# K on ScalarE's DMA queue, V and the queries on SyncE's: an attention kernel with one load queue or two

## The chip, the cores and the metric

The kernel runs on one core of one Trainium2 chip. A core has five engines with an instruction stream each: TensorE (PE, matrix products), VectorE (DVE), ScalarE (ACT), GpSimd (POOL) and SyncE (SP). They wait for each other on semaphores. Data comes from the chip's memory (HBM) into the on-chip buffer (SBUF) by 16 DMA engines; an instruction stream issues a transfer into its queue, the transfer is then spread over the 16 engines, and a semaphore tells when it has landed. The metric is the device time of one execution in microseconds (us); the number given is the median of the runs.

## The reference

```python
B, H, Sq, Skv, Dh = 8, 16, 16, 2048, 256        # q: B,H,Sq,Dh   k, v: B,H,Skv,Dh   all bf16

def reference(q, k, v):
    scale = q.shape[-1] ** -0.5
    scores = jnp.einsum('bhqd,bhkd->bhqk', q, k) * scale
    attn = _softmax(scores, axis=-1)
    return jnp.einsum('bhqk,bhkd->bhqd', attn, v)
```

There are 128 heads. Each has only 16 queries, but 2048 keys and values of 256 numbers. K and V are 134 MB each and are read once; queries and results are 1 MB each.

## The kernel before

**Tiles.** Eight heads make a group; there are G = 16 groups. The K of a group is loaded as four tiles of 2 MB, `K(4g)` to `K(4g+3)`, each 128 partitions by 32 tokens by 256 numbers, so that a partition reads 16 KB in one row. V is loaded in the same way as `V(4g)` to `V(4g+3)`. That gives NP = 64 loads of K and 64 of V. The last V is cut into four pieces of 16, 8, 4 and 4 tokens.

**Buffers.** `KN` holds raw K in R_KN = 3 slots, `KB` transposed K in R_KB = 3 slots, `VB` holds V in R_V = 5 slots. A load of K(i) waits until the second half of the transpose of K(i-3) is done; a load of V(j) waits until the product that uses V(j-5) is done.

**What happens to a group.** VectorE transposes a K tile in 32x32 blocks, in two halves (`kt`, L128). TensorE multiplies it with the prepared queries into the scores in PSUM (`qk`, L136, 8 products for each half). When all four tiles are in, VectorE takes the maximum (`max`, L142), ScalarE the exponentials in two halves (`exp`, L146), and VectorE transposes them (`pt`, L151) and forms the reciprocal of the sum (L348 to L351). TensorE multiplies with V (`pv`, L161): `pv(g,0)` uses V(4g) and V(4g+1), `pv(g,1)` the other two. ScalarE and VectorE scale and add the result (`evac_a`, L287, and `evac_b`, L295), and ScalarE issues the store of 64 KB (L176). The queries are loaded once (L228), and brought into the form that `qk` needs by TensorE (`qprep`, L113) and ScalarE (`qwb`, L121), two groups ahead.

**Order.** Each engine's stream is written out by hand as a list of jobs, and an engine does its jobs strictly in that order; `emit_stream` puts the waits in front of each. TensorE does, for group g: qk(4g), qk(4g+1), pv(g-1,0), qk(4g+2), qk(4g+3), pv(g-1,1), qprep(g+2). In the last group it does three qk ahead of pv(14,0), then qk(63) and pv(14,1), and then the last group's value products one tile at a time (`pv_last`, L170). ScalarE does, for group g: exp, qwb(g+2), evac_a(g-1), store(g-1). VectorE does kt(4g+1) to kt(4g+3), max(g), the first half of kt(4g+4), pt(g), the sums, the second half of kt(4g+4), and evac_b(g-1).

**Loads.** SyncE issues all loads, in the order of the list `seq`: K0, the queries, K1, K2, K3, and from then on K(i) followed by V(i-4). At the end the list runs K60, V56, K61, K62, V57, K63, V58 to V63. Since SyncE works in order, a K load that waits for its slot also holds up the V loads behind it.

Of the kernel before, what the change touches and what calls it, by code (L numbers as in the profile page):

```python
# [12 lines left out]
R_KN = 3  # L13
# [12 lines left out]
def bass_standalone__softmax_full_bidir__sampling_kernel(  # L26
# [11 lines left out]
    NP = 4 * G  # L38
# [7 lines left out]
    with ExitStack() as es:  # L46
# [30 lines left out]
        def J(eng, cls, emit, deps=(), dma=None):  # L77
            deps = [d for d in deps if d is not None]
            if dma is not None:
                jb = _Job(eng, cls, emit, deps, dma[0], dma[1], 16)  # L80
            else:
                if (eng, cls) not in counters:
                    counters[(eng, cls)] = [ec(nc.semaphore("c_%s_%s" % (eng, cls))), 0]
                c = counters[(eng, cls)]
                c[1] += 1
                jb = _Job(eng, cls, emit, deps, c[0], c[1])
            order[eng].append(jb)
            return jb
# [28 lines left out]
        def emit_qwb(eng, g):  # L117
            for a in range(4):
                dv = QW[32 * a:32 * a + 32, g % 2, 0, 0, :]
                sv = XP_ps[32 * a:32 * a + 32, 0, :]  # L120
                ins = eng.activation(ap_of(dv, dv.offset + 32 * a, [[8 * 128 + 1, 2], [128, 8], [2, 16]]),  # L121
                                     ap_of(sv, sv.offset + 16 * a, [[64, 2], [128, 8], [1, 16]]),
                                     ACTF.Copy, scale=scale)
            return ins
# [20 lines left out]
        def emit_exp(eng, g, h):  # L145
            return eng.activation(P_sb[:, 1024 * h:1024 * h + 1024],  # L146
                                  S_ps[:, 2 * h:2 * h + 2, :].rearrange("p c n -> p (c n)"), ACTF.Exp,
                                  bias=negm[:, g:g + 1], scale=1.0, accum_out=lsum[:, g, h:h + 1])
# [43 lines left out]
        for j in range(NP):  # L192
            g, r = j // 4, j % 4
            v_of.append((2 * g + r % 2, r // 2) if g < last else (2 * g + r // 2, r % 2))
        seq = []
        for i in range(NP):
            seq.append(("k", i))
            if i == 0:
                seq.append(("q", 0))
            if 4 <= i < NP - 3:  # L200
                seq.append(("v", i - 4))
            elif i == NP - 2:
                seq.append(("v", i - 5))
        seq += [("v", j) for j in range(NP - 6, NP)]

        j_k, j_v, j_kt, j_qk, j_pv = {}, {}, {}, {}, {}
        j_qwb, j_qprep, j_exp, j_pt, j_max, j_rab = {}, {}, {}, {}, {}, {}
# [2 lines left out]

        def k_load(i):
            s = i % R_KN
            return J("sp", "ld", lambda eng: eng.dma_start(
                KN[:, s], ku[i // 2, :, PT_TOK * (i % 2):PT_TOK * (i % 2) + PT_TOK, :]),
                [("kt", i - R_KN, 1) if i >= R_KN else None], dma=(sem_kn[s], 16 * (i // R_KN + 1)))

        def v_load(j, a, n, sem):
            s = j % R_V
            u, h = v_of[j]
            return J("sp", "ld", lambda eng: eng.dma_start(  # L220
                VB[:, s, a:a + n, :], vu[u, :, PT_TOK * h + a:PT_TOK * h + a + n, :]),
                [("pvuse", j - R_V) if j >= R_V else None], dma=sem)

        for what, i in seq:
            if what == "k":
                j_k[i] = k_load(i)
            elif what == "q":
                j_q = J("sp", "ld", lambda eng: eng.dma_start(QR[:], qg), dma=(sem_q, 16))  # L228
            elif i < NP - 1:
                j_v[i] = [v_load(i, 0, PT_TOK, (sem_v[i % R_V], 16 * (i // R_V + 1)))]  # L230
            else:
                parts, a = [], 0
                for x, n in enumerate(tail):
                    sem = ec(nc.semaphore("s_vt%d" % x))
                    parts.append(v_load(i, a, n, (sem, 16)))
                    a += n
                j_v[i] = parts
# [5 lines left out]
        def qwb(g):  # L243
            if g < G:
                j_qwb[g] = J("act", "qwb", lambda eng: emit_qwb(eng, g),
                             [("qprep", g), j_qwz, ("qk", 4 * g - 5, 1) if g >= 2 else None])
# [20 lines left out]
        def pv_last(r):  # L267
            g = last
            j = 4 * g + r
            u, h = v_of[j]  # L270
            a = 0
            for x, jv in enumerate(j_v[j]):
                n = PT_TOK if r < 3 else tail[x]
                j_pv["l", r] = J("pe", "pv", lambda eng, a=a, n=n: emit_pv1(
                    eng, g, u % 2, PT_TOK * h + a, PT_TOK * h + a + n, j % R_V, PT_TOK * h, g % 2 if u % 2 == 0 else 2),
                    [("pt", g, 0), ("pt", g, 1), ("eb", g - 2) if g >= 2 else None, jv])
                a += n

        def softmax_act(g):
            for h in range(2):  # L280
                j_exp[g, h] = J("act", "exp", lambda eng, h=h: emit_exp(eng, g, h),
                                [("max", g), ("pt", g - 1, h) if g else None])

        def evac_a(g):
            if g >= 0:
                dep = ("pvl", 1) if g == last else ("pv", g, 1)
                j_ea[g] = J("act", "ea", lambda eng: eng.activation(  # L287
                    O_tmp[:], O_ps[:, g % 2, 0:D], ACTF.Copy, scale=rab[:, g, 0:1]),
                    [dep, ("rab", g), ("eb", g - 1) if g else None])
# [9 lines left out]
        def store(g):  # L299
            if g >= 0:  # L300
                j_st[g] = J("act", "st", lambda eng: emit_store(eng, g), [("eb", g)],
                            dma=(sem_st[g % 2], 16 * (g // 2 + 1)))
# [19 lines left out]
        for r in range(4):  # L322
            if r == 3:
                J("pe", "warm", lambda eng: emit_warm(eng, 6), [("qwb", last)])
            pv_last(r)

        qwb(0)
        qwb(1)
        for g in range(G):
            softmax_act(g)  # L330
            qwb(g + 2)
            evac_a(g - 1)
            store(g - 1)
# [101 lines left out]
```

## Time and profile before

| | |
|---|---|
| runs | 656.22, 656.55, 656.96 us; median 656.55 |
| span of the profiled execution | 655.0 us |
| moved by the DMA | 271.34 MB, 414 GB/s over the span |
| SyncE's queue (q1) | 269.49 MB, 97.1% of 16 engines |
| ScalarE's queue (q10, the stores) | 1.05 MB, 0.6% |
| busy: TensorE, VectorE, ScalarE | 511.1, 376.3, 74.3 us |

The profiled execution has a span of 655.0 us from its first to its last instruction, 1.55 us less than the median of the runs. In the rows of groups, a row gives line, engine, operation, tiles and count, then the busy time and the mean time of one in ns, then the idle time of the engine just ahead of these instructions and what ended it. In rows of the timeline the first number is the start in us from the beginning of the span, the second the duration of the merged instructions, and brackets give the idle time ahead and what ended it. "SPq" and "ACTq" are instructions that issue a transfer on SyncE's or ScalarE's queue.

### The profile page before, as it was taken

The page shows a single profiled execution, that of the slowest core. Times are in us where ns is not written, and L with a number is a line of the kernel's source. Part 1 is how long each engine was busy: PE and PEld are TensorE (multiplying, and loading weights), DVE is VectorE, ACT ScalarE, POOL GpSimd, SP SyncE. Part 2 cuts the span into 40 slices and gives each one's busy share as a digit, 9 for nine tenths or more (in the row PEclk, how much of TensorE's full clock was granted, in tenths as well). Part 3 has the DMA queues.
Part 4 walks back from the last instruction along what each step waited for, and adds up shares of the span by engine and source line. Part 5 has one row for each costly group of instructions (what it writes and reads, how often), then busy time and mean ns, then how long its engine had stood idle before and what let it go on. Part 6 is the DMA issues. An engine that isn't in the chain of part 4 may idle for free.

```text
span 655.0 us, 12512 instructions
## 1 busy us (share of the span) xinstructions
PE 511.1 (78%) x5894; PEld 215.9 (33%) x5894; DVE 376.3 (57%) x242; ACT 74.3 (11%) x145; POOL 0.7 (0%) x6
## 2 busy tenths in 40 slices
PE   1868987867978777887878868689776878877886
PEld 1323332323333333332333323233322333322355
DVE  3884656557475573754746546574754837548520
ACT  2020201102011020200202002020200202001010
POOL 0000000000000000000000000000000000000000
PEclk9969988989988999888899979998998998879989
DMA  9999999999999999999999999999999999999982
GB/s 341 427 429 428 425 426 429 425 428 426 426 428 424 429 427 428 426 427 428 426 425 429 425 430 425 427 427 425 427 428 427 426 428 425 429 426 427 428 352 75
DMA packets 21747, 271.34 MB, mean 414 GB/s; under 512 B 2368, under 2 KB 4416, under 8 KB 5312
## 3 DMA queue, kind: packets, MB, share of 16 engines
q1 hardware_dynamic: 19392, 269.49, 97.1%
q10 hardware_dynamic: 2304, 1.05, 0.6%
q8 instruction: 46, 0.75, 0.5%
q14 instruction: 5, 0.04, 0.0%
HBM read 269.48 MB, written 1.05 MB: 413 GB/s over the span
## 4 chain that ended last, share of the span: by engine, by line
DMA 55%; PE 28%; DVE 12%; ACT 3%; issue 2%; SPq 0%; DVEq 0%
DMA KN<-in_k_dram 51%; PE O_ps L161 14%; PE S_ps L136 10%; DVE KB L128 10%; DMA VB<-in_v_dram 4%; ACT QW L121 2%; PE O_ps L170 2%; DVE negm L142 1%; DVE PT L151 1%; PE XP_ps L113 1%; ACT O_tmp L287 0%; PE XP_ps L180 0%; DVE rab L351 0%; DVE rinv L350 0%; DVE O_fin L295 0%
## 5 line engine op out<-in xcount | busy, mean ns | idle before, releaser
L128 DVE STREAM_TRANSPOSE KB<-KN 128x2048 f32<-128x2048 f32 x128 | 289.8, 2293 | 194.5 <-DMA KN<-in_k_dram 194.5
L136 PE MATMUL S_ps<-KB,QW 128*128 128x512 bf16 x1024 | 275.2, 422 | 120.4 <-DVE KB L128 119.2
L161 PE MATMUL O_ps<-VB,PT 32*32 32x512 bf16 x3840 | 214.0, 376 | 3.9 <-DMA VB<-in_v_dram 3.9
L136 PEld LDWEIGHTS S_ps<-KB,QW 128*128 128x128 bf16 x1024 | 99.3, 104 | 289.6 <-DVE KB L128 153.3
L161 PEld LDWEIGHTS O_ps<-VB,PT 32*32 32x32 bf16 x3840 | 94.9, 92 | 120.9 <-issue 18.4
L146 ACT ACTIVATE P_sb<-S_ps,negm 128x1024 bf16<-128x1024 f32 x32 | 35.4, 1110 | 497.4 <-DVE negm L142 497.4
L142 DVE TENSOR_REDUCE negm<-S_ps 128x1 f32<-128x2048 f32 x16 | 36.7, 2292 | 48.5 <-PE S_ps L136 48.5
L151 DVE STREAM_TRANSPOSE PT<-P_sb 128x1024 bf16<-128x1024 bf16 x32 | 37.3, 1204 | 1.3 <-ACT P_sb L146 1.3
L121 ACT ACTIVATE QW<-XP_ps 32x256 bf16<-32x256 bf16 x64 | 28.7, 448 | 48.8 <-PE XP_ps L113 48.2
L295 DVE SCALAR_TENSOR_TENSOR O_fin<-O_ps,rab,O_tmp 128x256 bf16<-128x256 f32 x16 | 7.5, 471 | 29.7 <-PE O_ps L170 18.0
L113 PE MATMUL XP_ps<-ident,QR 128*32 128x128 bf16 x512 | 10.9, 232 | 13.7 <-DMA QR<-in_q_dram 11.8
L170 PE MATMUL O_ps<-VB,PT 32*32 32x256 bf16 x512 | 14.8, 268 | 3.1 <-issue 3.1
L170 PEld LDWEIGHTS O_ps<-VB,PT 32*32 32x32 bf16 x512 | 13.2, 92 | 4.8 <-issue 4.1
L113 PEld LDWEIGHTS XP_ps<-ident,QR 128*32 128x32 bf16 x512 | 8.0, 102 | 19.9 <-DMA QR<-in_q_dram 11.8
L287 ACT ACTIVATE O_tmp<-O_ps,rab 128x256 f32<-128x256 f32 x16 | 7.6, 474 | 18.4 <-PE O_ps L161 10.2
L146 ACT ACTIVATION_READ_ACCUMULATOR P_sb<-S_ps,negm 128x1 f32 x32 | 6.3, 196 | 0.0
L351 DVE TENSOR_SCALAR rab<-mask,rinv 128x2 f32<-128x2 f32 x16 | 3.7, 229 | 0.6
L350 DVE RECIPROCAL rinv<-ltot 128x1 f32<-128x1 f32 x16 | 2.6, 164 | 0.5
L186 DVE MEMSET QW<- 128x2048 f32 x1 | 1.8, 1765 | 1.2 <-PEq L420 1.2
L348 DVE TENSOR_REDUCE ltot<-lsum 128x1 f32<-128x2 f32 x16 | 1.8, 113 | 0.0
L121 ACT ACT_TABLE_LOAD x1 | 1.3, 1283 | 3.1 <-DVE QW L186 3.1
L180 PE MATMUL XP_ps<-QR,ident 128*128 128x512 bf16 x6 | 1.5, 381 | 0.0
(8 smaller groups left out, 1.6 us busy)
## 6 DMA issues: line engine op xcount, KB each, us to landing
KN<-in_k_dram SPq DMA_DIRECT2D x64, 2048.0 KB, 24.9
VB<-in_v_dram SPq DMA_DIRECT2D x63, 2048.0 KB, 29.5
out_dram<-O_fin ACTq DMA_DIRECT2D x16, 64.0 KB, 9.5
VB<-in_v_dram SPq DMA_DIRECT2D x1, 1024.0 KB, 8.7
VB<-in_v_dram SPq DMA_DIRECT2D x1, 512.0 KB, 9.6
VB<-in_v_dram SPq DMA_DIRECT2D x2, 256.0 KB, 9.9
QR<-in_q_dram SPq DMA_DIRECT2D x1, 0.5 KB, 10.4
```

The source lines that it names most:

```text
L113: ins = eng.transpose(XP_ps[32 * a:32 * a + 32, bp, :], ap_of(qv, qv.offset + 64 * b + par, [[2, 32]]), ident[:], tile_position=(0, 32 * a))
L121: ins = eng.activation(ap_of(dv, dv.offset + 32 * a, [[8 * 128 + 1, 2], [128, 8], [2, 16]]), ap_of(sv, sv.offset + 16 * a, [[64, 2], [128, ...
L128: return eng.transpose(KBf[:, i % R_KB].rearrange("p t i -> p (t i)")[:, n * h:n * h + n], KNf[:, i % R_KN].rearrange("p t i -> p (t i)")[ ...
L136: ins = eng.matmul(S_ps[:, 2 * half + c, :], QW[:, g % 2, Gh, bp, :], ap_of(kb0, kb0.offset + 64 * b + par, [[D, 16], [2, 32]]), start=(Gh ...
L142: return eng.tensor_reduce(out=negm[:, g:g + 1], in_=S_ps[:].rearrange("p c n -> p (c n)"), axis=AX.X, op=ALU.max, negate=True)
L146: return eng.activation(P_sb[:, 1024 * h:1024 * h + 1024], S_ps[:, 2 * h:2 * h + 2, :].rearrange("p c n -> p (c n)"), ACTF.Exp, bias=negm[ ...
L151: return eng.transpose(PT[:, g % 2].rearrange("p t x -> p (t x)")[:, 1024 * h:1024 * h + 1024], P_sb[:, 1024 * h:1024 * h + 1024])
L161: ins = eng.matmul(O_ps[pr, g % 2, :], PT[pr, g % 2, t, :], rhs, start=(t == 0), stop=(t == NT - 1), tile_position=(32 * a, 32 * a))
L170: ins = eng.matmul(O_ps[pr, bank, D * Gh:D * Gh + D], PT[pr, g % 2, t, :], VB[pr, s, t - base, :], start=(t == 0), stop=(t == NT - 1), til ...
L287: j_ea[g] = J("act", "ea", lambda eng: eng.activation(O_tmp[:], O_ps[:, g % 2, 0:D], ACTF.Copy, scale=rab[:, g, 0:1]), [dep, ("rab", g), ( ...
L295: j_eb[g] = J("dve", "eb", lambda eng: eng.scalar_tensor_tensor(out=O_fin[:, g % 2, :], in0=O_ps[:, bank, D:2 * D], scalar=rab[:, g, 1:2], ...
L351: j_rab[g] = J("dve", "sm", lambda eng, g=g: eng.tensor_scalar(out=rab[:, g, :], in0=mask[:], scalar1=rinv[:, g:g + 1], scalar2=None, op0= ...
```

## The change

All 64 K loads are issued by ScalarE, and so go into ScalarE's queue, in which the stores are already. SyncE issues the queries and the 64 V loads (67 with the last one's pieces). The slots and semaphores stay: three for raw K, five for V, and each load waits for the same use of its slot as before. There is no order any more between K loads and V loads.

In ScalarE's stream K0, K1 and K2 come first. For group g, the loads up to K(4g+6) are issued ahead of the exponentials, K(4g+7) behind them, and then follow qwb(g+2), evac_a(g-1) and store(g-1) as before. K(4g+7) waits for the second half of kt(4g+4). So the store of group g-1 stands in ScalarE's queue between K(4g+7) and K(4g+8).

```diff
-        seq = []
-        for i in range(NP):
-            seq.append(("k", i))
-            if i == 0:
-                seq.append(("q", 0))
-            if 4 <= i < NP - 3:
-                seq.append(("v", i - 4))
-            elif i == NP - 2:
-                seq.append(("v", i - 5))
-        seq += [("v", j) for j in range(NP - 6, NP)]
+        seq = [("q", 0)] + [("v", j) for j in range(NP)]
...
         def k_load(i):
             s = i % R_KN
-            return J("sp", "ld", lambda eng: eng.dma_start(
+            return J("act", "ld", lambda eng: eng.dma_start(
                 KN[:, s], ku[i // 2, :, PT_TOK * (i % 2):PT_TOK * (i % 2) + PT_TOK, :]),
                 [("kt", i - R_KN, 1) if i >= R_KN else None], dma=(sem_kn[s], 16 * (i // R_KN + 1)))
...
         for what, i in seq:
-            if what == "k":
-                j_k[i] = k_load(i)
-            elif what == "q":
+            if what == "q":
                 j_q = J("sp", "ld", lambda eng: eng.dma_start(QR[:], qg), dma=(sem_q, 16))
...
+        for i in range(R_KN):
+            j_k[i] = k_load(i)
         qwb(0)
         qwb(1)
+        nk = R_KN
         for g in range(G):
+            while nk < min(4 * g + 7, NP):
+                j_k[nk] = k_load(nk)
+                nk += 1
             softmax_act(g)
+            if nk < NP and nk == 4 * g + 7:
+                j_k[nk] = k_load(nk)
+                nk += 1
             qwb(g + 2)
             evac_a(g - 1)
             store(g - 1)
```

## The prediction

> **What bounds the kernel now.** I read the page first: the slices, the DMA queues and the chain that ended last.
>
> ```profile
> span 655.0 us, 12512 instructions
> DMA  9999999999999999999999999999999999999982
> GB/s 341 427 429 428 425 426 429 425 428 426 426 428 424 429 427 428 426 427 428 426 425 429 425 430 425 427 427 425 427 428 427 426 428 425 429 426 427 428 352 75
> q1 hardware_dynamic: 19392, 269.49, 97.1%
> q10 hardware_dynamic: 2304, 1.05, 0.6%
> DMA 55%; PE 28%; DVE 12%; ACT 3%; issue 2%; SPq 0%; DVEq 0%
> ...
> L128 DVE STREAM_TRANSPOSE KB<-KN 128x2048 f32<-128x2048 f32 x128 | 289.8, 2293 | 194.5 <-DMA KN<-in_k_dram 194.5
> L287 ACT ACTIVATE O_tmp<-O_ps,rab 128x256 f32<-128x256 f32 x16 | 7.6, 474 | 18.4 <-PE O_ps L161 10.2
> KN<-in_k_dram SPq DMA_DIRECT2D x64, 2048.0 KB, 24.9
> VB<-in_v_dram SPq DMA_DIRECT2D x63, 2048.0 KB, 29.5
> out_dram<-O_fin ACTq DMA_DIRECT2D x16, 64.0 KB, 9.5
> ```
>
> The reader is to see that the transfers are the bound from end to end: 37 slices in a row are full, at 424 to 430 GB/s, and VectorE, which uses K first, sits 194.5 us waiting for it. A load of 2048 KB is 2.097 MB, so at 427 GB/s one load takes 4.91 us, and a K arrives 24.9 us, five loads, after its issue: the queue is never dry. Next I asked for busy time by stretches of the span (PE, PEld, DVE, ACT, POOL, then granted clock, DMA share, GB/s) and for the waits of SyncE's queue.
>
> ```profile
> 0.00:16.00 16.00, 2.32 (x65) 1.69 (x66) 6.42 (x4) 3.22 (x6) 0.70 (x6) 1.00 0.92 342
> 560.00:600.00 40.00, 32.84 (x320) 12.91 (x320) 24.03 (x16) 2.78 (x5) 0.00 (x0) 0.87 1.01 426
> 620.00:638.00 18.00, 14.14 (x317) 9.04 (x315) 5.58 (x7) 2.78 (x5) 0.00 (x0) 0.91 0.88 361
> 638.00:655.00 17.00, 10.96 (x338) 8.62 (x332) 0.48 (x1) 0.47 (x1) 0.00 (x0) 0.99 0.23 85
> SPq L213 <- DVE KB L128: 537.9, 61, 13.1
> SPq L220 <- PE O_ps L161: 34.2, 3, 18.2
> ```
>
> In the middle the share is 1.01: no gap is left for a second queue to fill. SyncE waits nearly always for a K slot (537.9 us) and hardly ever for a V slot (34.2 us, 3 times). So today V is loaded in the order that the list gives it, not as early as its slots allow. Only the end is not full, and there the order decides. Hence the last view, the timeline of the end.
>
> ```profile
> 579.05 4.50 DVE L128 STREAM_TRANSPOSE KB<-KN 128x2048 f32<-128x2048 f32 x2 [5.28 <-DMA KN<-in_k_dram]
> 587.48 7.08 PE L161 MATMUL O_ps<-VB,PT 32*32 32x512 bf16 x128
> 613.42 4.50 DVE L128 STREAM_TRANSPOSE KB<-KN 128x2048 f32<-128x2048 f32 x2 [5.37 <-DMA KN<-in_k_dram]
> 616.97 3.66 PE L136 MATMUL S_ps<-KB,QW 128*128 128x512 bf16 x16
> 624.49 8.53 PE L161 MATMUL O_ps<-VB,PT 32*32 32x512 bf16 x128 [3.86 <-DMA VB<-in_v_dram]
> 652.10 0.48 DVE O_fin L295
> ```
>
> Rows one and three are the arrivals of K59 (579.05) and K63 (613.42). At K59 the list has delivered K0 to K59 and V0 to V54: 115 loads. At K63 it has delivered 64 K and V0 to V57: 122 loads, and 7 x 4.91 = 34.4 us lie between, as measured. The last-but-one value product, pv(14,1), starts at 624.49, when V59 is there (124 loads). From there TensorE has its own work up to 652.10 (27.6 us), while the DMA has little left (85 GB/s after 638), and 2.9 us follow for the last evacuation and store. So the end is the start of pv(14,1) plus 30.5 us, and what the change does to that start is the answer.
>
> **The change part by part.** Bytes, number of transfers and every compute instruction stay. Removed: 64 K issues on SyncE. Added: 64 K issues on ScalarE. Moved: V and the queries are no longer held behind K.
>
> *The issues on ScalarE.* One costs 0.33 us, and the new places wait for kt(4g+4,1), a transpose behind which ScalarE's qwb, evac_a and store now stand.
>
> ```profile
> 300.83 4.50 DVE L128 STREAM_TRANSPOSE KB<-KN 128x2048 f32<-128x2048 f32 x2 [5.28 <-DMA KN<-in_k_dram]
> 316.14 1.83 ACT L121 ACTIVATE QW<-XP_ps 32x256 bf16<-32x256 bf16 x4 [2.96 <-PE XP_ps L113]
> 318.05 0.33 SPq L213 DMA_DIRECT2D KN<-in_k_dram  x1
> 318.55 0.48 DVE L295 SCALAR_TENSOR_TENSOR O_fin<-O_ps,rab,O_tmp 128x256 bf16<-128x256 f32 x1 [0.54 <-issue]
> 320.62 4.51 DVE L128 STREAM_TRANSPOSE KB<-KN 128x2048 f32<-128x2048 f32 x2 [1.58 <-DMA KN<-in_k_dram]
> 2.21 5.89 SPq L213 DMA_DIRECT2D KN<-in_k_dram  x1
> ```
>
> Today qwb runs at 316.14. Behind the issue at 318.05 it would run at 318.4, evac_a (0.47) at 320.2, and VectorE's evac_b (today 318.55) at about 320.7 to 321.2, 2.5 us later, where the next transpose starts 0.6 us late. VectorE sits idle 194.5 / 16 = 12 us per group, and the transfers do not stop for it: price 0. If that cover were gone it would be 0.6 to 2.5 us per group, 10 to 40 us. The K issues ahead of the exponentials wait only for transposes that the maximum needs anyhow: 0. An issue can block: the one behind the queries took 5.89 us. On ScalarE at most three loads stand in the queue, fewer than the five that SyncE held at 0.33 us an issue; price 0, upper bound 5.6 us in a group, still under the 12 us.
>
> *The start.* All of K0 to K2, the queries and V0 to V4 are issued at once, so K shares the engines with V. Whatever is fetched first, the engines stay full: six K fit ahead of the first use of the queries (three raw slots, three transposed), 6 x 4.91 = 29 us, and then five V, 25 us. How late can the queries be? Today 11.78 us:
>
> ```profile
> 11.78 1.05 PE L113 MATMUL XP_ps<-ident,QR 128*32 128x128 bf16 x32 [11.78 <-DMA QR<-in_q_dram]
> DMA to landing us min/median/max: 1.9/9.5/10.4
> ```
>
> If they are starved by K, at the latest when those six K are in and their ring is alone, at about 36 us. No byte is lost: price 0, with 0 to 3 us in the range.
>
> *The share of each queue, the main term.* The second row above is for the 16 stores. Alone at the end one lands in 1.9 us; beside the loads it takes 9.5 for 64 KB. q10's 2304 packets are 9 per store and DMA engine (128 rows and 16 completions over 16 engines): 7.6 us for nine, 0.84 each, near the time in which an engine moves one 16 KB row of a load, 4.91 / 8 = 0.61. So a small packet takes a turn as a large one does. By that, K and V get half each while both have work. But the stores stay on ScalarE's queue, and now stand in one line with K: each holds K for nine turns, some 5.5 us, in which V gets 1.1 loads more. That repeats in each group, so V runs ahead until its five slots are full, within two or three groups, and from then on idles briefly before each value product. The Trainium skill, "DMA: Bandwidth & Descriptors", section "Queues, rings and completion order", has the engines alternate between rings after packets of typically 9 to 17 descriptors; then a store would be about one turn and V's gain an estimated 1 to 2 loads, and as the slots are the limit, the sum would be the same. No row here separates the two.
>
> *What it does to the end.* With V full ahead, when K59 arrives only V57 and V58, freed for loading by pv(13,0) just then, are missing: 60 K and V0 to V56, 117 loads in place of 115. The engines being full, K59 arrives 2 x 4.91 = **9.8 us later**, at 588.9. Bounds: V55 must be there for pv(13,1) 8.4 us after K59 (587.48), so at least 56 - 8.4 / 9.82 = 55.1 V, hence +0.6 us; slots allow 57. I take 57 because of the stores.
>
> From K59's arrival (0): pv(13,1) ends at 15.5, as today (587.48 + 7.08), and V59 and V60 flow from 17.4 (plus 1.9). Till then 3.55 loads come: V57, V58 and 1.55 K. K62 needs 1.45 more at half rate, 14.2 us: 31.6. K63 needs all eight loads: 39.3. qk(62) ends 4.5 + 1.83 (half of 3.66) after K62: 37.9. pv(14,0): 45.0. qk(63), whose transpose ended at 43.8: 48.7. There pv(14,1) starts, all its V being long there; today 624.49 - 579.05 = 45.4. So **+3.3 us**: today's list brings K61 and K62 back to back and K63 ahead of the last six V, and that order is gone.
>
> pv(14,1) took 8.53 us behind an idle of 3.86 with the clock down; without the idle I take the 7.08 of the other rows: **-1.45 us**. V61 and V62 (issued at 45.0) and V63 (at 55.8) come while TensorE works through the other last products. V63 is needed last, 23 us after pv(14,1) starts, at 72, and lands by about 66:
>
> ```profile
> 633.06 1.97 SPq L220 DMA_DIRECT2D VB<-in_v_dram  x4
> ```
>
> Its four issues take 1.97 us and its load 4.91 + 1.9. The DMA idles some 8 us after K63, but the end does not wait for that.
>
> **Sum:** 9.8 + 3.3 - 1.45 = +11.7 us on this execution's 655.0 us span. The median of the runs is 656.55 (1.5 us around the span): **668.2 us**, 1.8% slower.
>
> **The rivals.**
> *Even shares, no push by the stores* (packets of a store pass in the shadow of V's). V stays between 55.1 and 57 at K59; at 56: +4.9. K60 to K63 then come every 9.82 us, K62 at 29.5, K63 at 39.3; pv(14,0) ends at 42.9, qk(63) at 45.6: +0.2, less 1.45: **660.2 us**. For it: loads are all alike in size. Against: the 9.5 us.
> *Nothing moves*: the engines are as full either way, K63 comes as early as now: **656.5 us**. For it: share 1.01 before. The Trainium skill, same page, section "Issuing engines are not separate DMA queues", says that several issuers only save issue time; the trace agrees that there is no bandwidth to win (427 GB/s, full slices). Against: today's 34.2 us of V waits show that order, not slots, limits V, and that order is dropped.
> *Faster: K's queue gets more than half.* V then lags, K fills its slots, and K63 is there early; pv(14,1) starts as soon as 124 loads are in, 613.42 + 2 x 4.91 = 623.2, 1.3 us before today, and 1.45 come from the clock: **653.8 us**. It decides if K63 lands before about 617 (623.2 less 4.5 and 1.83). For it: SyncE's queue starts with the queries' many small rows and a blocked issue (5.89 us). Against: the stores in K's line.
> *Worse: ScalarE's longer line stops the transfers.* If an issue blocks as it did at 2.21 and evac_b with it, beyond VectorE's 12 us, each us per group is 16 us: **684 us** at one. Against: K's issues in the middle, 0.33 us each.
>
> **How the numbers follow.** V full ahead 0.48 (662.5 to 673); even shares 0.20; nothing moves 0.07; K favoured 0.13; ScalarE the brake 0.12. The range 657 to 674 leaves out the faster case and most of the last. About 0.2% (1.3 us) can be told from no change: faster 0.13, same 0.07, slower 0.80. The likeliest case's own range, 662.5 to 673, takes in a V count of 56.3 and the start's 3 us.
>
> **What the changed profile would show.** Full slices at 424 to 430 GB/s up to about 622; SyncE's waits all for value products (L161), hundreds of us; stores landing in about 20 us in place of 9.5, behind K; K59 at about 589, K63 at 628; V58 to V60 landed before K63, then a dip in GB/s; pv(14,1) without a wait for V at 637.6 or so. K59 at 583 would mean even shares. The forecast is wrong if the slices in the middle drop or rise (the rate depends on the queues), if V is still late for pv(14,1), or if VectorE waits for evac_a (L287) long enough to leave both queues dry.

## The result: 1.4% slower, and the profile after

The changed kernel takes 666.25 us (median; 662.35 to 669.38), the kernel before 656.61 us. The ratio is 1.014, with a 95% interval from 1.010 to 1.018. The forecast was 668.2 us in a range of 657 to 674, slower.

The page of the changed kernel, in the lines that answer to those shown of before. K's loads are now in q10, with the stores, V's and the queries' in q1; the profiled execution took 665.1 us.

```profile
span 663.0 us, 12511 instructions
DMA  8999999999999999999999999999999999999672
GB/s 355 417 426 429 426 426 430 424 427 426 427 428 426 426 426 429 427 428 427 429 424 427 426 429 429 424 428 424 428 426 414 427 427 428 427 427 424 278 303 89
q10 hardware_dynamic: 11520, 135.27, 48.4%
q1 hardware_dynamic: 10176, 135.27, 48.2%
L128 DVE STREAM_TRANSPOSE KB<-KN 128x2048 f32<-128x2048 f32 x128 | 289.6, 2293 | 176.2 <-DMA KN<-in_k_dram 176.2
out_dram<-O_fin ACTq DMA_DIRECT2D x16, 64.0 KB, 17.3
```

The middle is as full as before and at the same rate, 424 to 430 GB/s but for one slice of 414: here a second queue brings no bandwidth and costs hardly any. The end differs. The third slice from the right is at 278 GB/s where it was at 428, and more is left for the last two. A store lands 17.3 us after its issue, not 9.5: it stands in line with K.

Who waits has changed as well. This is the view of the waits of SyncE's queue:

```profile
SPq L211 <- PE O_ps L161: 602.6, 30, 62.1
```

V now waits for a free slot all the time (602.6 us; 34.2 us before). Each V load is issued as early as the five slots allow. The timeline of the end shows what that does; the rows are K59, K62 and K63 arriving, TensorE's scores and products behind them, and the last evacuation.

```profile
589.30 4.50 DVE L128 STREAM_TRANSPOSE KB<-KN 128x2048 f32<-128x2048 f32 x2 [4.68 <-DMA KN<-in_k_dram]
618.73 4.50 DVE L128 STREAM_TRANSPOSE KB<-KN 128x2048 f32<-128x2048 f32 x2 [2.07 <-DMA KN<-in_k_dram]
625.13 7.08 PE L161 MATMUL O_ps<-VB,PT 32*32 32x512 bf16 x128
627.87 4.50 DVE L128 STREAM_TRANSPOSE KB<-KN 128x2048 f32<-128x2048 f32 x2 [4.63 <-DMA KN<-in_k_dram]
632.15 3.66 PE L136 MATMUL S_ps<-KB,QW 128*128 128x512 bf16 x16
635.74 7.08 PE L161 MATMUL O_ps<-VB,PT 32*32 32x512 bf16 x128
660.16 0.48 DVE L284 SCALAR_TENSOR_TENSOR O_fin<-O_ps,rab,O_tmp 128x256 bf16<-128x256 f32 x1 [16.23 <-PE O_ps L170]
```

K59 arrives at 589.30 (before 579.05), K63 at 627.87 (before 613.42), and pv(14,1), in the row at 635.74, starts 11.25 us later than before. From its start to the end of the span it takes 27.3 us, where it took 30.5.

What pv(14,1) waits for is seen in the chain that ended last (start, duration, what):

```profile
593.83 24.87 DMA KN<-in_k_dram
...
623.29 1.91 PE S_ps L136 x8
625.20 7.01 PE O_ps L161 x128
632.22 3.59 PE S_ps L136 x16
635.81 7.01 PE O_ps L161 x128
```

The chain leaves the transfers with K62, which lands at 618.7. Behind it come K62's transpose and scores, then pv(14,0), which stands ahead of qk(63) in TensorE's order, then K63's scores and pv(14,1), without a break. K63 is not on the chain: its two halves were transposed by 630.2 and 632.4, and TensorE, busy with pv(14,0), came to them at 632.2 and about 634. Before, pv(14,1) waited for V59, and K62 arrived long ahead of that, at 603.55:

```profile
603.55 4.50 DVE L128 STREAM_TRANSPOSE KB<-KN 128x2048 f32<-128x2048 f32 x2 [0.43 <-DMA KN<-in_k_dram]
```

So K62 is 15.18 us later, at 4.91 us a load about three loads. As the number of K loads ahead of it is fixed, these are V loads.

### The profile page after: what moved, and what is told of

Same layout as the page of the kernel before. It is cut to its first block, busy times and chain, and to the rows that moved or that the text cites. A ratio compares the mean times of both kernels' runs of the same rounds, so it can differ in the third digit from the quotient of the medians.

```text
span 663.0 us, 12511 instructions
## 1 busy us (share of the span) xinstructions
PE 515.1 (78%) x5893; PEld 216.2 (33%) x5894; DVE 376.0 (57%) x242; ACT 74.4 (11%) x145; POOL 0.7 (0%) x6
## 5 line engine op out<-in xcount | busy, mean ns | idle before, releaser
L128 DVE STREAM_TRANSPOSE KB<-KN 128x2048 f32<-128x2048 f32 x128 | 289.6, 2293 | 176.2 <-DMA KN<-in_k_dram 176.2
L136 PE MATMUL S_ps<-KB,QW 128*128 128x512 bf16 x1024 | 280.5, 429 | 120.0 <-DVE KB L128 119.3
L136 PEld LDWEIGHTS S_ps<-KB,QW 128*128 128x128 bf16 x1024 | 100.7, 105 | 293.6 <-DVE KB L128 152.2
## 6 DMA issues: line engine op xcount, KB each, us to landing
out_dram<-O_fin ACTq DMA_DIRECT2D x16, 64.0 KB, 17.3
QR<-in_q_dram SPq DMA_DIRECT2D x1, 0.5 KB, 20.7
```

The lines of the kernel that those rows point to most:

```text
L128: return eng.transpose(KBf[:, i % R_KB].rearrange("p t i -> p (t i)")[:, n * h:n * h + n], KNf[:, i % R_KN].rearrange("p t i -> p (t i)")[ ...
L136: ins = eng.matmul(S_ps[:, 2 * half + c, :], QW[:, g % 2, Gh, bp, :], ap_of(kb0, kb0.offset + 64 * b + par, [[D, 16], [2, 32]]), start=(Gh ...
```

## The experiments

The theory to be tested had three parts. First, the transfers are full either way, so that what counts is how many V loads land ahead of the last K loads (the order). The expectations speak of K63; on the chain of the change it is K62. Second, V gets ahead because the stores in K's line push it, up to its slots. Third, ScalarE's longer line and the second queue cost nothing in themselves. The main rival was that the split itself costs.

**One queue, with only the order altered.** The kernel before, all loads on SyncE; K63 is moved behind V60.

```diff
         seq += [("v", j) for j in range(NP - 6, NP)]
+        seq.remove(("k", NP - 1))
+        seq.insert(seq.index(("v", NP - 3)), ("k", NP - 1))
```

> The kernel before, with one queue on SyncE, and only the list altered: K63 is loaded behind V58, V59 and V60 in place of ahead of them. Order theory (what the change costs is the number of V loads that land ahead of K63): K59 as before at 579 us, K63 at 628 us (three loads later), pv(14,1) at 635 to 636 us, and the time of the change without any second queue: 663 to 667 us. Rival (two queues cost in themselves): clearly less, under 660 us.

Measured: 667.11 us, ratio 1.0153 (1.0140 to 1.0167). The timeline of this run: K59 and K63 arriving, K63's scores, pv(14,1).

```profile
578.98 4.50 DVE L128 STREAM_TRANSPOSE KB<-KN 128x2048 f32<-128x2048 f32 x2 [5.29 <-DMA KN<-in_k_dram]
...
629.15 4.50 DVE L128 STREAM_TRANSPOSE KB<-KN 128x2048 f32<-128x2048 f32 x2 [21.13 <-DMA KN<-in_k_dram]
...
631.51 6.57 PE L136 MATMUL S_ps<-KB,QW 128*128 128x512 bf16 x16 [14.51 <-DVE KB L128]
638.02 7.08 PE L161 MATMUL O_ps<-VB,PT 32*32 32x512 bf16 x128
```

K59 is where it was before, and everything up to it is the old kernel. Yet the time is that of the change. So three V loads ahead of one of the last K are enough for a loss of this size, with one queue, no issue on ScalarE and no lead in the middle. The path differs, though: here K62 was early, pv(14,0) was done before K63 came, and pv(14,1) waits for K63 itself; in the change it waits for K62. The time is just above the expectation: pv(14,1) starts 2 us later, since the scores took 6.57 us after 14.51 us of idle of TensorE. That it agrees with the change to within 1 us is in part luck.

**Two queues, only the end held back.** V runs ahead freely until V57, which waits for K61; V58 to V63 wait for K62.

```diff
+        def gate(j):
+            return ("kl", min(j + 4, NP - 2)) if j >= NP - 7 else None
+
...
-                [("pvuse", j - R_V) if j >= R_V else None], dma=sem)
+                [("pvuse", j - R_V) if j >= R_V else None, gate(j)], dma=sem)
...
-        tables = {"kt": j_kt,
+        tables = {"kl": j_k, "kt": j_kt,
```

> Two queues as in the change, V runs ahead as far as its slots allow through the whole kernel; only V57 waits until K61 has landed, and V58 to V63 until K62 has landed. Theory of the end (the lead itself costs nothing, what costs is that V59 and V60 are loaded ahead of K63, so that K63's transposes and scores stand behind the last wait): K59 still at about 589 us, but K63 at about 617 us, pv(14,1) starts at 623 to 625 us, and the time is 652 to 656 us. Rival (the 9.8 us by which K59 comes later are lost for good): pv(14,1) at 634 us or later, 662 us or more.

Measured: 657.64 us, ratio 1.0016 (1.0007 to 1.0024). K59, the transposes of K61 and K62, K63, and pv(14,1) in the timeline:

```profile
588.72 4.50 DVE L128 STREAM_TRANSPOSE KB<-KN 128x2048 f32<-128x2048 f32 x2 [3.63 <-DMA KN<-in_k_dram]
...
607.36 8.88 DVE L128 STREAM_TRANSPOSE KB<-KN 128x2048 f32<-128x2048 f32 x4
...
622.08 4.50 DVE L128 STREAM_TRANSPOSE KB<-KN 128x2048 f32<-128x2048 f32 x2 [5.84 <-DMA KN<-in_k_dram]
...
628.74 7.08 PE L161 MATMUL O_ps<-VB,PT 32*32 32x512 bf16 x128
```

K59 is as late as in the change (588.72), and still 8.6 of the 9.6 us come back. The lead in the middle is not lost time; it is lost only if V goes on ahead of the last K. The expectations of K63, of pv(14,1) (by some 4 us) and of the time were missed all the same. Behind a late K59 VectorE's own work sets the pace: K61 and K62 are transposed without a break up to 616.2, and pv(14,0) and K63's scores follow.

**The stores.** Twice the 16 stores were taken out of K's line: into a queue of GpSimd's own, and into SyncE's, behind V.

```diff
-                j_st[g] = J("act", "st", lambda eng: emit_store(eng, g), [("eb", g)],
+                j_st[g] = J("pool", "st", lambda eng: emit_store(eng, g), [("eb", g)],
```

> The 16 stores are issued by GpSimd into a queue of their own, so they hold up neither K nor V more than the other. Push theory: between the change and the run with the stores in V's line; V is not pushed ahead, K59 lands at 582 to 586 us, K63 at 618 to 624 us, and the time is 658 to 663 us. Rival (any relief of K's line is enough, V falls back fully): like the run with the stores in V's line, 656 to 658 us. Rival (V runs ahead without the stores): K59 at 588 us or later and 664 us or more.

Measured: 661.97 us, ratio 1.0081 (1.0066 to 1.0096). The timeline (K59, K62, K63, pv(14,1)):

```profile
584.15 4.51 DVE L128 STREAM_TRANSPOSE KB<-KN 128x2048 f32<-128x2048 f32 x2 [5.28 <-DMA KN<-in_k_dram]
...
613.73 4.50 DVE L128 STREAM_TRANSPOSE KB<-KN 128x2048 f32<-128x2048 f32 x2 [5.24 <-DMA KN<-in_k_dram]
...
623.48 4.50 DVE L128 STREAM_TRANSPOSE KB<-KN 128x2048 f32<-128x2048 f32 x2 [5.25 <-DMA KN<-in_k_dram]
...
632.03 7.08 PE L161 MATMUL O_ps<-VB,PT 32*32 32x512 bf16 x128
```

```diff
-                j_st[g] = J("act", "st", lambda eng: emit_store(eng, g), [("eb", g)],
+                j_st[g] = J("sp", "st", lambda eng: emit_store(eng, g), [("eb", g)],
...
+            if what == "v" and i >= 8 and i % 4 == 0:
+                store(i // 4 - 2)
+        store(last - 1)
+        store(last)
...
-            store(g - 1)
...
-        store(last)
```

> The 16 stores go to SyncE's queue, behind V(4g+8), so that they hold up V and not K. Push theory (the stores in K's line drive V ahead until its five slots are full): V falls back by about one load per group to what the value products need, K59 lands 0.6 to 5 us after the kernel before instead of 10.3 us (so between 580 and 584 us in the profile), and the time is 657 to 661 us. Rival (V runs ahead because five slots allow it, and stores do not matter): K59 stays near 589 us and the time near 666 us.

Measured: 657.93 us, ratio 1.0014 (1.0004 to 1.0024). The timeline: the two value products of group 13, which wait for V, and K63.

```profile
574.86 8.52 PE L161 MATMUL O_ps<-VB,PT 32*32 32x512 bf16 x128 [2.72 <-DMA VB<-in_v_dram]
...
594.44 8.77 PE L161 MATMUL O_ps<-VB,PT 32*32 32x512 bf16 x128 [3.98 <-DMA VB<-in_v_dram]
...
614.78 4.50 DVE L128 STREAM_TRANSPOSE KB<-KN 128x2048 f32<-128x2048 f32 x2 [1.68 <-DMA KN<-in_k_dram]
```

The medians from issue to landing, of the change and of the run with the stores in V's line:

```profile
KN<-in_k_dram ACTq DMA_DIRECT2D x64, 2048.0 KB, 22.3
VB<-in_v_dram SPq DMA_DIRECT2D x63, 2048.0 KB, 23.2
...
KN<-in_k_dram ACTq DMA_DIRECT2D x64, 2048.0 KB, 17.7
VB<-in_v_dram SPq DMA_DIRECT2D x63, 2048.0 KB, 34.3
```

So the place of 1 MB of stores among 269 MB of loads shifts which of the two runs ahead. In K's line, V leads, and K62 lands at 618.73 and K63 at 627.87; in neither line, at 613.73 and 623.48; in V's line, K leads, K63 lands at 614.78, and now products wait for V. There K was further ahead than expected: its tiles before K60 are transposed without a wait, so that K59's landing can't be read. With the stores in neither line K62 is one load earlier than in the change, and still two loads later than before (603.55): the stores push V by about one of the three loads, and the other two come with the order that the one queue kept and two do not. With the stores in GpSimd's queue K62 and K63 are 9.75 us apart, twice 4.9: there K and V shared the engines evenly. In GpSimd's queue a store is also cut differently, 512 packets in all where ScalarE's had 2304, so that part of the relief may be fewer turns.

**Four V slots.**

```diff
-R_V = 5
+R_V = 4
```

> V has four slots in place of five, nothing else changes. Lead theory (each V load that lands ahead of need costs its 4.91 us, and K63 comes last): V lands one load less ahead, K59 at about 584 us, K63 at about 623 us, the product pv(14,1) starts at about 631 us, and the time is 660 to 662 us. Rival (the time is lost by the split itself, by ScalarE's longer line or by the lack of slots): 666 us or more, with slices under 424 GB/s in the middle.

Measured: 667.37 us in the median of six executions, two at 658.19 and 660.39 and four from 666.97 to 669.62. The profiled one (660.39 us) had K59 at 583.91, as expected. Its K62, K63 and pv(14,1), the last two ahead of the expectation:

```profile
609.12 4.50 DVE L128 STREAM_TRANSPOSE KB<-KN 128x2048 f32<-128x2048 f32 x2 [2.16 <-DMA KN<-in_k_dram]
...
618.88 4.51 DVE L128 STREAM_TRANSPOSE KB<-KN 128x2048 f32<-128x2048 f32 x2 [5.26 <-DMA KN<-in_k_dram]
...
627.37 7.08 PE L161 MATMUL O_ps<-VB,PT 32*32 32x512 bf16 x128
```

The four others were no better than the change. A further execution was one of that kind.

> The kernel with four V slots once more, whose executions lie at 658 to 660 or at 667 to 670 us: in a slow one the lead theory expects full slices in the middle and a late K59 (592 us or so); a dry-queue rival expects slices in the middle that fall under 420 GB/s, eight us of transfer time in all.

Measured: 665.93 us. Its timeline (K59, K62, K63, pv(14,1)):

```profile
581.00 4.50 DVE L128 STREAM_TRANSPOSE KB<-KN 128x2048 f32<-128x2048 f32 x2 [5.28 <-DMA KN<-in_k_dram]
...
615.36 4.50 DVE L128 STREAM_TRANSPOSE KB<-KN 128x2048 f32<-128x2048 f32 x2 [5.29 <-DMA KN<-in_k_dram]
...
623.69 4.50 DVE L128 STREAM_TRANSPOSE KB<-KN 128x2048 f32<-128x2048 f32 x2 [3.83 <-DMA KN<-in_k_dram]
...
633.37 7.08 PE L161 MATMUL O_ps<-VB,PT 32*32 32x512 bf16 x128
```

Neither expectation held. K59 is *earlier* than in the quicker execution and yet pv(14,1) is 6 us later, because K62 is 6.24 us later: by its size, about one V load more landed ahead of it. K63 is 4.81 us later, but in neither execution does TensorE wait for it, since pv(14,0) is not yet done when its transpose ends. K59 alone says little; K62 says it. What makes an execution go one way or the other was not settled.

**All V in the old order, on two queues.** Each V load also waits for the transpose that frees the slot of the K load ahead of it in the old list.

```diff
+        def gate(j):
+            return ("kt", min(j + 1 if j < 57 else j + 2, NP - 4), 1)
...
-                [("pvuse", j - R_V) if j >= R_V else None], dma=sem)
+                [("pvuse", j - R_V) if j >= R_V else None, gate(j)], dma=sem)
```

> Two queues as in the change, but each V load also waits for the transpose that frees the K slot for the K load ahead of it in the old list, so that V is issued in the old order. Lead theory: K59 lands at 579 to 581 us as before the change, K63 later than before (621 us in place of 613, as it shares with V58), pv(14,1) starts at about 628 us, and the time is 655 to 658 us. Rival (the split itself costs): 663 to 667 us, though V is no longer ahead.

Measured: 659.42 us, ratio 1.0037 (1.0024 to 1.005): most of the loss is gone, but the time is above the expectation, and K59 was at 588.33 and not at 580 in the profiled execution (662.85 us, the slowest of six). The page and a stretch of the middle (PE, PEld, DVE, ACT, POOL, clock, DMA share, GB/s) show why:

```profile
GB/s 354 389 427 392 429 426 428 425 424 427 426 430 426 426 426 428 429 392 427 429 427 427 420 427 428 429 427 409 427 425 428 429 406 428 430 425 425 423 331 84
281.00:298.00 17.00, 11.23 (x152) 4.40 (x140) 9.22 (x10) 4.54 (x9) 0.00 (x0) 0.90 0.94 392
```

Five slices fall to 389, 392, 392, 409 and 406. Against 427 they lack 147 GB/s for 16.5 us each, some 5.7 us of transfers: now both queues wait for the same transposes, and at times, it seems, both are dry. So the freedom of V is worth something too: in the change, where V does not wait for the transposes, the middle stays full.

**The start.** K3 and K4 are issued ahead of the first query preparations.

```diff
-        for i in range(R_KN):
+        nk = R_KN + 2
+        for i in range(nk):
             j_k[i] = k_load(i)
         qwb(0)
         qwb(1)
-        nk = R_KN
```

> K3 and K4 are issued ahead of the first two query preparations, so that K3 no longer waits for the queries. Theory (the transfers are full at the start whatever is fetched first): K3 lands at about 27 to 30 us in place of 40.5, the queries at up to 30 us in place of 21.6, and the time stays at that of the change, 663 to 668 us. Rival (the late K3 starts the lag that is seen at the end): K59 at 584 us or earlier and 661 us or less.

Measured: 665.8 us, as the change; the queries took 26.2 us in place of 20.7. K3's transpose starts at 34.67 us in place of 40.52, held by TensorE and not by the load, so K3's landing can't be read. So the late K3 of the change costs nothing.

**The change once more**, to see why its executions differ.

> The changed kernel once more, to see where executions of it differ (662 to 669 us): if they differ by how far V is ahead, K59 lands at another time than 589.3 us and the end moves by the same; if they differ by the tail, K59 stays at 589 us and the time from pv(14,1) on differs from 27 us.

Measured: 667.92 us, span 665.8. K63 lands at 627.67, 0.2 us from the first profile, though K59 was at 584.74: neither branch of the expectation. pv(14,1) starts 2.7 us later than in the first profile: 0.4 us from K62's landing (619.14), 2.3 us from K62's scores. The rows are, of this execution, those scores and a stretch around them (PE, clock, DMA share, GB/s):

```profile
621.51 6.38 PE L136 MATMUL S_ps<-KB,QW 128*128 128x512 bf16 x16 [5.70 <-DVE KB L128]
621.00:628.00 7.00, 6.49 (x20) 0.56 0.49 205
```

and of the first profile of the change:

```profile
621.10 1.91 PE L136 MATMUL S_ps<-KB,QW 128*128 128x512 bf16 x8 [2.47 <-DVE KB L128]
623.29 1.91 PE L136 MATMUL S_ps<-KB,QW 128*128 128x512 bf16 x8 [0.28 <-DVE KB L128]
621.00:626.00 5.00, 4.62 (x32) 1.00 0.53 222
```

After 5.70 us of idle the granted clock was 0.56, after 2.47 it was 1.00. In the changed kernel this stands on the path, since pv(14,0) and K63's scores are behind it.

**Both mends together**, the stores on GpSimd's queue and the gate at the end (the edits above).

> Both mends together: stores on GpSimd's queue, and V57 waits for K61, V58 to V63 for K62. K59 at 582 to 586 us; the end is then set by VectorE's chain of work behind K59, which took 40.0 us up to pv(14,1) in the run with the gate alone: pv(14,1) at 623 to 626 us, and 653 to 657 us in time, about that of the kernel before or a little under. Rival (the transfers stop for lack of issues, as at the end of the run with the gate alone, and K63 is late again): 658 us or more.

Measured: 657.74 us, ratio 1.0019 (1.0010 to 1.0028). K59 at 584.21, K63 at 616.50, pv(14,1) at 625.10, as expected, and yet a little over the expected time and slower than before: the two mends don't add up. pv(14,1) is close to 623.2, when by the prediction's sum the 124 loads up to V59 are in, and behind it the tail takes its 27 to 30 us (30.4 here, to the end of the 655.5 us span), which no run here touched. No version beat the kernel before.

## Why the prediction was right, point by point

**Where the last K land** is the sound part. K63 was predicted at 628.2 and measured at 627.87 and 627.67; the sum behind it is 125 loads of 4.91 us with the engines full (64 K and V0 to V60), and one queue with the same 125 loads gave 629.15. The forecast's path to pv(14,1) was right too: K62, its scores, pv(14,0), and K63's scores with no wait for K63. K62 was predicted at 620.5 and measured at 618.73 and 619.14.

**The split into 9.8 and 3.3 us** was less sound. K59 was predicted at 588.9 and measured at 589.30 in the first profile, but at 584.74 in the second, with the same K63. How far V leads at K59 wanders, and K59 near 583, which the forecast gave as the sign of even shares, can't tell the cases apart. "+9.8 us for K59" and "+3.3 us for the end" are one term, three V loads ahead of K62: it is 15.18 us later than before in the first profile and 15.59 in the second, and pv(14,1) less than that, as it waited for V59 before. In the first profile the two parts were 10.25 and 1.0 (46.44 from K59 to pv(14,1) in place of 45.44), in the second 5.7 and 8.2.

**The push by the stores** held in direction: without it K62 lands 5 us earlier and 4.3 us come off the time, and with the stores in V's line K is in the lead. K59 does not show it, as it is at 584.15 without the push and was at 584.74 with it, in the second profile. What did not hold is that the push must fill all slots in every execution, and it gives about one of the three loads.

**pv(14,1)** was predicted at 637.6, by the offsets from K59, and measured at 635.74 and 638.43. In the first profile the miss is K62's landing, 1.8 us early. In the second that is nearly made up by 2.3 us of K62's scores at a lower clock, which the forecast did not have; that it came so close there is luck.

**The tail term** was mis-sized. -1.45 us was predicted for pv(14,1) at full clock; it did take 7.08 us, but the tail shrank by 3.2. Most of the rest lies in TensorE's gaps in the last products: 1.11 and 1.97 us before, 1.29 and 0.06 after. Why the second gap closes was not tried. Sum in the first profile: 10.25 + 1.0 - 3.2 = 8.0 us, the difference of the spans (663.0 and 655.0).

**ScalarE's line, price 0**, held: VectorE's wait for K went from 194.5 to 176.2 us, so the later evacuations came out of idle time, and the run with the end held back has all of ScalarE's issues and is 0.16% from the kernel before. **The start, price 0**, held too, but its working missed a wait: K3 was issued at 25.6 us, behind the query preparations on ScalarE, and not when its slot was free.

**The rivals.** "Even shares" at 660.2 us is close to what the run with the stores on GpSimd's queue took (661.97). "K favoured" was predicted at 653.8; the run with the stores in V's line took 657.93, as V's lag cost waits. "Nothing moves" fell, and so did "ScalarE the brake" at 684 us. The Trainium skill, "DMA: Bandwidth & Descriptors", section "Issuing engines are not separate DMA queues", was borne out on bandwidth (427 GB/s in the middle, before and after), but the step from there to an unchanged time fails: a second queue drops the order between the two streams, and that costs 1.4%.

## What to carry to other kernels

When transfers are the bound and full, as here, moving loads to another queue does not make them faster; it changes who arrives last. So find in the chain that ended last the load with which it leaves the transfers (here K62, and not K63, which comes after it), count the loads that land ahead of that one, and multiply. An order written into one queue can carry the end of a kernel: if it is split, hold back at the end what is not needed next, which gave back all but 0.16% here. Look at what else stands in a queue: here small stores in the line of one of two streams pushed the other one ahead.

## What had not been expected of the hardware

The queries, a load of small packets in a queue beside K's large ones, slowed K by a fifth and were themselves slowed to double: they took 20.7 us to land, where they took 10.4 in one queue with K (before). The start of the changed kernel in its timeline, K0 to K2 arriving and the issue behind the queries':

```profile
8.59 4.50 DVE L128 STREAM_TRANSPOSE KB<-KN 128x2048 f32<-128x2048 f32 x2 [5.45 <-DMA KN<-in_k_dram]
14.52 4.50 DVE L128 STREAM_TRANSPOSE KB<-KN 128x2048 f32<-128x2048 f32 x2 [1.43 <-DMA KN<-in_k_dram]
20.47 4.50 DVE L128 STREAM_TRANSPOSE KB<-KN 128x2048 f32<-128x2048 f32 x2 [1.44 <-DMA KN<-in_k_dram]
1.70 5.82 SPq L211 DMA_DIRECT2D VB<-in_v_dram  x1
```

K0 to K2 arrived at 8.59, 14.52 and 20.47 us while the queries were loaded beside them, 5.95 us for a load that takes 4.91 at the full rate. That fits turns by packet and not by byte: 27 packets of K on each DMA engine and 33 of the queries (528 by q1's count of before, less 144 for each of its 131 V and K loads, over 16). And the issue that follows the queries in their queue took 5.82 us, for V0 on SyncE, as K1's did before (5.89 us).
